# Gated linear attention ahead of two expert layers: gate sums on TensorE, whole query and score tiles, no products on GpSimd

## The chip, the cores and the metric

The kernel runs on one core of one Trainium2 chip. The metric is the time of one execution on the device in microseconds (us); the kernel before takes 743.27 us, the median of three runs between 742.84 and 743.48. In the profile the engines are called PE (TensorE, PEld its weight loads), DVE (VectorE), ACT (ScalarE), POOL (GpSimd) and SP (SyncE, which issues most DMAs).

## The reference

Three things are computed one after the other: a gated linear attention, and two top-1 expert layers on its rows. Only the first is touched.

```python
# q, k, v, f_logit: batch 4, heads 8, 768 tokens, 48 wide
f = 1.0 / (1.0 + np.exp(-f_logit))
for t in range(S):
    state = f[:, :, t, :, None] * state + einsum('bhd,bhe->bhde', k[:, :, t], v[:, :, t])
    y[:, :, t] = einsum('bhd,bhde->bhe', q[:, :, t], state)
x = y.transpose(0, 2, 1, 3).reshape(3072, 384)
x = moe(x, 8 experts, 384 -> 1024 -> 384, capacity)    # top-1, gated
x = moe2(x, 8 experts, 384 -> 1024 -> 384)             # top-1, gated
```

## The kernel before

The attention goes through 24 tiles of 128 tokens (six a batch), all eight heads of a tile at a time. A tile lies transposed: four head pairs beside each other, in each pair one head's 48 channels in partitions 0 to 47 and the other's in 64 to 111, the 128 tokens along the free axis. `X` holds gates, keys and queries of a tile in this form (3 x 4 x 128 float32 per partition); `Vn` and `R` hold the values in two natural layouts.

For a tile, with G the running sum of log(1 + exp(-f)) over its tokens, the chunked form is: `gates` (ScalarE) makes `L` = ln(1 + exp(-f)) in two activations; `decay` (VectorE) adds it up along the tokens with one scan (L372), held under a limit by the tile `caps` (L369); `expand` (ScalarE, L387 and L388) makes `eg` = exp(-G) and `ei` = exp(G). Queries times `eg` and keys times `ei` are the factors: the first head's query product (L389) and the key product `KD` (L390) on GpSimd, the second head's query product on VectorE in `keys` (L396). The first two tiles have L389 on VectorE, too. `T` is one tile of two planes, one for each head of a pair: the 64 partitions of the head hold its queries, the other 64 get its masked scores. `keys_t` transposes `KD` on TensorE and ScalarE copies it (`KT`); `scores` multiplies `KD` and `T` in quadrants of 64x64 (L416, L417), `masked` brings them through the causal mask into the other half of `T` in two instructions of 64x512 (L423); `updates` multiplies `KT` with `Vn` (`kv`), `states` (VectorE, L452 and L461) carries the state `S` on. `place` copies the states into `R` beside the values (ScalarE, L471 and L472), so that one product of 128 rows per head and chunk, 64x48 (L482), gives states and scores together in `y`. `rows`, `rows_t`, `rows_c` and `logits` copy the rows out, transpose them (`xp`, `xT`) and multiply by the gate weights (`rt`, L254).

The loop of 27 steps is software pipelined. The table `STAGES` gives the order in which a step issues its stages and how many tiles each lags behind; every engine runs its own instructions in that order. Per three tiles the routing adds some twenty tiny VectorE instructions (the one-hot choice `dla`, `oha`, the counts `cum`, the slots), which `step()` puts between the large ones. The weights of the first expert are split in two parts, `w0h` and `w0l`, on the way (`SPLITS`: behind which step, on which engine). SP issues all loads in order; X has four buffers, Vn three, R four.

After the loop a hand-written tail works off the last tiles and the first products of the first expert (`hpm`), and then both expert layers run as one sequence of groups, on TensorE mostly. If a chunk's decay leaves a safe range (`_guard`) a general path recomputes everything; it doesn't run here.

Of the kernel before, what the change touches and what calls it, by code (L numbers as in the profile page):

```python
# [22 lines left out]
DM = H * D  # L23
# [16 lines left out]
GMAX = 40.0  # L40
GCLAMP = 80.0
# [26 lines left out]
C_W = 360  # L68
# [125 lines left out]
def _route(*args, **kw):  # L194
# [9 lines left out]
# The engine of the weight splits behind a loop step of the attention: v(ector) or g(psimd).  # L204
SPLITS = {7: "v", 9: "g", 12: "g", 14: "g", 18: "g", 21: "g", 23: "g", 24: "v", 26: "gvvv"}
# Products by loop step that keep the tensor engine clocked up while the attention starts.
NWARM = (11, 1, 0, 0, 0, 11, 7, 3, 0, 0)

# What a loop step of the attention does, in each engine's order, and how many tiles behind.
STAGES = (  # L210
    ("place", 6),
    ("g_choose", 9),
    ("g_save", 13),
    ("decay", 3),
# [13 lines left out]
    ("keys", 3),  # L228
# [12 lines left out]
# in the first NFIRST steps with the next tile's gates behind the tile's own factors  # L241
# [4 lines left out]
# tiles with query factors from the vector engine, and tiles whose gates are loaded by themselves  # L246
NDVE = 2
NSPLIT = 2
# [16 lines left out]
def _scatter1(tc, key, dst, idx, src, bound):  # L265
    """Rows to places of their own: no two scatters of a key write the same row."""
    ins = tc.nc.gpsimd.indirect_dma_start(  # L267
        out=dst,
        out_offset=bass.IndirectOffsetOnAxis(ap=idx, axis=0),
        in_=src,  # L270
        in_offset=None,
        bounds_check=bound,
        oob_is_err=False,
    )
    ins = ins.ins
    tc.declare_no_dep(ins, group=key, reason="scatters to distinct rows")
    tc.add_to_no_dep_group(key, ins)
# [13 lines left out]
def _attention(tc, env, fkq, vn, vs, x1, tab1, early, masks, first, side, after, first_group):  # L291
    """Chunked attention, a tile of 128 tokens (two chunks) for all heads at a time, and the routing
    of its rows. Software pipelined: each loop step works on seven tiles, a stage apart."""
    nc = tc.nc
    with ExitStack() as ctx:
# [15 lines left out]
        caps = [e1.tile([P, NPAIR, P], F32, name=f"caps{i}") for i in range(2)]  # L311
        for c in caps:
            nc.vector.memset(c, GCLAMP)
        NVB = 3
        NXB = 4
        xbuf = [e1.tile([P, 3, NPAIR, P], F32, name=f"X{i}") for i in range(NXB)]
        tbuf = [b1.tile([P, 2, NPAIR, P], F32, name=f"T{i}") for i in range(4)]
        vbuf = [b1.tile([P, 2, DM], F32, name=f"Vn{i}") for i in range(NVB)]
        for vb in vbuf:
            nc.gpsimd.memset(vb[64:128, 0], 0.0)  # L320

        def load_x(i):
            t = tiles[i] = _Bag()
            t.X = xbuf[i % NXB]
            if i < NSPLIT:
                nc.sync.dma_start(out=t.X[:, 0], in_=fkq[i, :, 0])
                if i == 1:
                    masks()
                nc.sync.dma_start(out=t.X[:, 1:3], in_=fkq[i, :, 1:3])
            elif i < NXB:  # L330
                nc.sync.dma_start(out=t.X, in_=fkq[i])
# [11 lines left out]
        def load_vs(i):  # L343
            t = tiles[i]
            t.R = b4.tile([P, 2, 2, NPAIR * D], F32, name=f"R{i}", tag="R")
            nc.sync.dma_start(out=t.R[64:128, :, 0, :], in_=vs[i, 0])
            nc.sync.dma_start(out=t.R[0:64, :, 1, :], in_=vs[i, 1])

        # the first tile in halves, a step of each behind the other
        halves = lambda i: [slice(0, 2), slice(2, NPAIR)] if i == 0 else [slice(0, NPAIR)]  # L350

        def gates(i):
            t = tiles[i]
            t.L = e2.tile([P, NPAIR, P], F32, name=f"L{i}", tag="L")
            En = e2.tile([P, NPAIR, P], F32, name=f"En{i}", tag="En")
            for k, a in enumerate(halves(i)):
                col = NTILE if k else i
                nc.scalar.activation(
                    flat(En[:, a]), flat(t.X[:, 0, a]), AF.Exp, scale=-1.0, accum_out=env.esum[:, col : col + 1]
                )  # L360
                nc.scalar.activation(flat(t.L[:, a]), flat(En[:, a]), AF.Ln, bias=1.0)

        def decay(i):
            t = tiles[i]
            t.G = e2.tile([P, NPAIR, P], F32, name=f"G{i}", tag="G")
            # sums up to the limit; where a head pair starts, the limit is its own first term
            c = caps[i % 2]
            for a in halves(i):
                nc.vector.tensor_scalar(  # L369
                    out=c[:, a, 0:1], in0=t.L[:, a, 0:1], scalar1=GCLAMP, scalar2=None, op0=ALU.min  # L370
                )
                nc.vector.tensor_tensor_scan(  # L372
                    out=flat(t.G[:, a]), data0=flat(t.L[:, a]), data1=flat(c[:, a]), initial=0.0, op0=ALU.add, op1=ALU.min
                )
            step()
            step()

        def expand(i):
# [3 lines left out]
            t.T = tbuf[i % 4]  # L382
            t.KD = b2.tile([P, NPAIR, P], F32, name=f"KD{i}", tag="KD")
            # at first nothing else has work
            eng = nc.vector if i < NDVE else nc.gpsimd
            for a in halves(i):
                nc.scalar.activation(flat(t.eg[:, a]), flat(t.G[:, a]), AF.Exp, scale=-1.0)  # L387
                nc.scalar.activation(flat(t.ei[:, a]), flat(t.G[:, a]), AF.Exp)  # L388
                eng.tensor_tensor(out=t.T[0:64, 0, a], in0=t.X[0:64, 2, a], in1=t.eg[0:64, a], op=ALU.mult)  # L389
                nc.gpsimd.tensor_tensor(out=t.KD[:, a], in0=t.X[:, 1, a], in1=t.ei[:, a], op=ALU.mult)  # L390
            nc.gpsimd.tensor_copy(out=env.glast[:, i], in_=t.G[:, :, P - 1])

        def keys(i):
            t = tiles[i]
            for a in halves(i):
                nc.vector.tensor_tensor(  # L396
                    out=t.T[64:128, 1, a], in0=t.X[64:128, 2, a], in1=t.eg[64:128, a], op=ALU.mult
                )
# [1349 lines left out]
```

## Time and profile before

| what | us |
|---|---|
| time, median of three runs | 743.27 |
| span of the profiled execution | 737.6 |
| PE busy in the span | 664.8 |
| DVE busy | 467.8 |
| POOL busy | 393.2 |
| ACT busy | 327.9 |

The span goes from the first to the last instruction of the profiled execution; the time also takes in what lies around it. Busy times are of the whole span, in which the attention (to about 180 us) and the expert layers have different limits, so the rows below are taken by stretch. A busy TensorE is not one at its peak, and instructions that wait at a port count as busy.

### The profile page before, as it was taken

Reading aid. Unit: us, or ns where it says so; the run is one execution under the profiler, and the core shown is the slowest. Engines: PE = TensorE matmul, PEld = TensorE weight load, DVE = VectorE, ACT = ScalarE, POOL = GpSimd, SP = SyncE. Lnnn points to the kernel's source line nnn. Section 1 sums busy time; section 2 is a strip of 40 time slices with the busy share of each in tenths; the row PEclk is TensorE's granted clock in tenths of the full one; section 3 lists DMA queues with packets and bytes.
Section 4 is the critical chain, followed back from the end, with each engine's and each line's share of the span. In section 5 each row is a group of like instructions: output and inputs, shape, how many; then the busy total and the mean of one; then the engine's idle time right before and its main releaser. Section 6 shows DMA issues by size and latency. Waiting matters only on the chain.

```text
span 737.6 us, 15364 instructions
## 1 busy us (share of the span) xinstructions
PE 664.8 (90%) x5583; PEld 607.6 (82%) x5586; DVE 467.8 (63%) x1036; ACT 327.9 (44%) x702; POOL 393.2 (53%) x368
## 2 busy tenths in 40 slices
PE   7777686777889999999999899979999999999995
PEld 4556575666779899989999799869999899999995
DVE  8999999998558655574465755425545353555642
ACT  6566666665225443434434244115444343454431
POOL 4354757555446654645737454136765475756731
PEclk9899878789899999999999999999999999999998
DMA  9999999932348664655748161127544354544400
GB/s 265 247 213 212 180 188 199 168 101 80 93 115 221 183 160 98 152 87 169 147 144 171 48 204 40 31 74 252 152 136 127 105 159 121 164 141 134 130 23 20
DMA packets 61175, 104.27 MB, mean 141 GB/s; under 512 B 12444, under 2 KB 30462, under 8 KB 61091
## 3 DMA queue, kind: packets, MB, share of 16 engines
q1 hardware_dynamic: 53411, 87.63, 48.3%
q0 software_dynamic: 7680, 15.57, 7.7%
q8 instruction: 46, 0.75, 0.5%
q14 instruction: 38, 0.31, 0.2%
HBM read 88.21 MB, written 15.79 MB: 141 GB/s over the span
## 4 chain that ended last, share of the span: by engine, by line
PE 54%; DVE 19%; DMA 13%; issue 8%; POOL 2%; SPq 2%; ACT 1%; another core or an unknown queue 0%; DVEq 0%; POOLq 0%
PE hpm L1131 24%; PE ypm L1155 7%; PE ypm L1156 7%; PE ypm L1157 7%; DMA out_dram<-yr,tdm 5%; DVE T L396 4%; DVE T L423 3%; DMA X<-in_fkq_dram 3%; PE tpm L1108 2%; DVE dla L103 2%; DVE G L372 1%; DVE xT L511 1%; DMA raw<-in_w_dram 1%; DMA Vn<-in_vn_dram 1%; PE tym L896 1%
## 5 line engine op out<-in xcount | busy, mean ns | idle before, releaser
L1131 PE MATMUL hpm<-xhm,w0h 128*128 128x288 f32 (+11 forms) x456 | 155.6, 342 | 4.4 <-DVE hlm L1143 3.6
L1155 PE MATMUL ypm<-hhm,w1h 128*128 128x288 f32 (+11 forms) x456 | 155.0, 340 | 0.0
L1143 DVE SCALAR_TENSOR_TENSOR hlm<-hpm,hhm 128x288 fp32r<-128x288 f32 (+11 forms) x152 | 81.4, 536 | 115.7 <-ACT hhm L1142 89.3
L1156 PE MATMUL ypm<-hlm,w1h 128*128 128x288 f32 (+11 forms) x456 | 151.3, 332 | 0.0
L1157 PE MATMUL ypm<-hhm,w1l 128*128 128x288 f32 (+11 forms) x456 | 150.9, 331 | 0.0
L1142 ACT ACTIVATE hhm<-hpm 128x288 fp32r<-128x288 f32 (+11 forms) x152 | 72.5, 477 | 176.1 <-PE hpm L1131 160.9
L1131 PE MATMUL hpm<-xhm,w0l 128*128 128x288 f32 (+11 forms) x456 | 150.8, 331 | 0.0
L1131 PE MATMUL hpm<-xlm,w0h 128*128 128x288 f32 (+11 forms) x456 | 145.0, 332 | 0.0
L996 POOL TENSOR_TENSOR w0l<-raw,w0h 128x512 fp32r<-128x512 f32 x63 | 80.2, 1289 | 51.9 <-ACT w0h L995 51.4
L281 POOL DMA_INDIRECT xrm<-x,idcm x64 | 70.2, 1097 | 54.9 <-DVE valm L991 34.1
L996 POOL TENSOR_TENSOR w1l<-raw,w1h 128x512 fp32r<-128x512 f32 x60 | 77.0, 1298 | 34.6 <-ACT w1h L995 33.6
L1131 PEld LDWEIGHTS hpm<-xhm,w0h 128*128 128x128 f32 x456 | 86.8, 190 | 7.6 <-DVE hlm L1143 4.2
L1155 PEld LDWEIGHTS ypm<-hhm,w1h 128*128 128x128 f32 x456 | 86.9, 191 | 2.0
L1157 PEld LDWEIGHTS ypm<-hhm,w1l 128*128 128x128 f32 x456 | 86.7, 190 | 2.2
L1156 PEld LDWEIGHTS ypm<-hlm,w1h 128*128 128x128 f32 x456 | 86.9, 190 | 1.8
L1131 PEld LDWEIGHTS hpm<-xhm,w0l 128*128 128x128 f32 x456 | 86.7, 190 | 1.7
L1131 PEld LDWEIGHTS hpm<-xlm,w0h 128*128 128x128 f32 x456 | 85.6, 190 | 2.2
L267 POOL DMA_INDIRECT tab<-pos,sum x30 | 30.6, 1019 | 67.8 <-DVE sum L176 61.4
L389 POOL TENSOR_TENSOR T<-X,eg 64x512 f32<-64x512 f32 x22 | 28.2, 1283 | 63.7 <-ACT eg L387 55.1
L1116 ACT CAST xhm<-tpm 128x336 fp32r<-128x336 f32 (+8 forms) x64 | 25.2, 435 | 79.9 <-PE tpm L1108 76.8
L995 ACT CAST w0h<-raw 128x512 fp32r<-128x512 f32 x96 | 57.2, 616 | 2.5 <-DMA raw<-in_w_dram 2.3
L995 ACT CAST w1h<-raw 128x512 fp32r<-128x512 f32 x96 | 56.4, 621 | 0.0
(201 smaller groups left out, 1133.6 us busy)
## 6 DMA issues: line engine op xcount, KB each, us to landing
raw<-in_w_dram SPq DMA_DIRECT2D x192, 256.0 KB
X<-in_fkq_dram SPq DMA_DIRECT2D x40, 288.0 KB
x<-xr SPq DMA_DIRECT2D x8, 582.0 KB
Vn<-in_vn_dram SPq DMA_DIRECT2D x24, 192.0 KB
R<-in_vs_dram SPq DMA_DIRECT2D x48, 96.0 KB
Vn<-in_vn_dram SPq DMA_DIRECT2D x24, 96.0 KB
X<-in_fkq_dram SPq DMA_DIRECT2D x2, 768.0 KB
X<-in_fkq_dram SPq DMA_DIRECT2D x2, 512.0 KB
```

What stands on the lines that cost most here:

```text
L267: ins = tc.nc.gpsimd.indirect_dma_start(out=dst, out_offset=bass.IndirectOffsetOnAxis(ap=idx, axis=0), in_=src, in_offset=None, bounds_che ...
L281: nc.gpsimd.indirect_dma_start(out=dst, out_offset=None, in_=src, in_offset=bass.IndirectOffsetOnAxis(ap=idx, axis=0), bounds_check=bound, ...
L389: eng.tensor_tensor(out=t.T[0:64, 0, a], in0=t.X[0:64, 2, a], in1=t.eg[0:64, a], op=ALU.mult)
L396: nc.vector.tensor_tensor(out=t.T[64:128, 1, a], in0=t.X[64:128, 2, a], in1=t.eg[64:128, a], op=ALU.mult)
L995: nc.scalar.copy(out=hi, in_=raw)
L996: eng.tensor_tensor(out=lo, in0=raw, in1=hi.bitcast(F32), op=ALU.subtract)
L1131: nc.tensor.matmul(hp[:, :N], w[:, c, fs], x[:, c, :N], start=(k == 0), stop=(k == len(parts) - 1))
L1142: nc.scalar.activation(hh[:, :N], hp[:, :N], AF.Relu)
L1143: nc.vector.scalar_tensor_tensor(out=hl[:, :N], in0=hp[:, :N], scalar=0.0, in1=hh[:, :N].bitcast(F32), op0=ALU.max, op1=ALU.subtract)
L1155: nc.tensor.matmul(g.yp[d][:, :N], w2h[:, fc, ds_], hh[:, :N], start=(fc == 0), stop=False)
L1156: nc.tensor.matmul(g.yp[d][:, :N], w2h[:, fc, ds_], hl[:, :N], start=False, stop=False)
L1157: nc.tensor.matmul(g.yp[d][:, :N], w2l[:, fc, ds_], hh[:, :N], start=False, stop=(fc == NFC - 1))
```

## The change

- **Gate sums.** The gate inputs come untransposed, 128 tokens in the partitions (`F`, 192 KB a tile, a DMA of its own, three buffers). A new stage `bound` on VectorE holds them above -80. The two activations of `gates` run on 384 columns instead of 512. `sums` on TensorE replaces `decay`: four products per tile with a triangular matrix of ones (`C_INC` in the constants) leave G transposed in PSUM, in the same two buffers (tag `tr`) that the transposes `kp` and `xp` use. The scan and `caps` go.
- **Factors.** `factors` on VectorE makes the whole query tile `QT` (128x512) and the whole key tile `KD` (128x512, with ei held under a limit in the same instruction). `expand` keeps its two activations, now from PSUM; GpSimd's products and the stage `keys` go. GpSimd keeps the small copy `glast`.
- **Scores and outputs.** The scores of both heads stay in their own quadrants, and `masked` is one instruction of 128x512 into a tile `SC`. The output has, per pair and chunk, one product of `QT` with block-diagonal states `RS` and one of `SC` with block-diagonal values `RV`, 64x96 each, added up in PSUM: sixteen products of 96 columns in place of sixteen of 48. The zero blocks are set once by GpSimd memsets at the start; `RS` has two buffers, `RV` three.
- **Splits.** All twelve weight splits of the attention are on GpSimd, one behind each of the steps 7, 9, ... 23, 24, 25, 26; four were on VectorE, three of these behind step 26.
- **Small things.** No halves for the first tile; the constants `cs` grow from 360 to 488 columns and are loaded behind the first gates; the guard compares exp(-G).

The core of the diff (removed comments and unchanged stages left out):

```diff
-SPLITS = {7: "v", 9: "g", 12: "g", 14: "g", 18: "g", 21: "g", 23: "g", 24: "v", 26: "gvvv"}
+SPLITS = {7: "g", 9: "g", 11: "g", 13: "g", 15: "g", 17: "g", 19: "g", 21: "g", 23: "g", 24: "g", 25: "g", 26: "g"}
 STAGES = (
     ("place", 6),
+    ("bound", 2),
...
-    ("decay", 3),
+    ("sums", 3),
...
-    ("keys", 3),
+    ("factors", 3),
...
+        fbuf = [e1.tile([P, DM], F32, name=f"F{i}") for i in range(3)]
+        xbuf = [e1.tile([P, 2, NPAIR, P], F32, name=f"X{i}") for i in range(NXB)]
+        sbuf = [b1.tile([P, 2, 2, NPAIR * D], F32, name=f"RS{i}") for i in range(2)]
+        rbuf = [b1.tile([P, 2, 2, NPAIR * D], F32, name=f"RV{i}") for i in range(NRB)]
...
+            nc.sync.dma_start(out=t.F, in_=fn[i])
...
                 for u in (0, 64):
-                    nc.sync.dma_start(out=t.X[u : u + D], in_=fkq[i, u : u + D])
+                    nc.sync.dma_start(out=t.X[u : u + D], in_=kq[i, u : u + D])
...
+        def bound(i):
+            t = tiles[i]
+            nc.vector.tensor_scalar(out=t.F, in0=t.F, scalar1=FMIN, scalar2=None, op0=ALU.max)
...
-                nc.vector.tensor_tensor_scan(
-                    out=flat(t.G[:, a]), data0=flat(t.L[:, a]), data1=flat(c[:, a]), initial=0.0, op0=ALU.add, op1=ALU.min
-                )
+            t.G = p_2.tile([P, NPAIR, P], F32, name=f"G{i}", tag="tr")
+            for a in range(NPAIR):
+                nc.tensor.matmul(
+                    t.G[:, a],
+                    t.L[:, 2 * a : 2 * a + 2].rearrange("p h d -> p (h d)"),
+                    env.cs[:, C_INC : C_INC + P],
+                    start=True,
+                    stop=True,
                 )
...
-                eng.tensor_tensor(out=t.T[0:64, 0, a], in0=t.X[0:64, 2, a], in1=t.eg[0:64, a], op=ALU.mult)
-                nc.gpsimd.tensor_tensor(out=t.KD[:, a], in0=t.X[:, 1, a], in1=t.ei[:, a], op=ALU.mult)
+        def factors(i):
+            t = tiles[i]
+            t.QT = b4.tile([P, NPAIR, P], F32, name=f"QT{i}", tag="QT")
+            t.KD = e2.tile([P, NPAIR, P], F32, name=f"KD{i}", tag="KD")
+            nc.vector.tensor_tensor(out=t.QT, in0=t.X[:, 1], in1=t.eg, op=ALU.mult)
             step()
+            nc.vector.scalar_tensor_tensor(
+                out=t.KD, in0=t.ei, scalar=EIMAX, in1=t.X[:, 0], op0=ALU.min, op1=ALU.mult
+            )
             step()
...
+                    for q in (slice(0, 64), slice(64, 128)):
+                        nc.tensor.matmul(sc[q, a, h], t.KD[q, a, u], t.QT[q, a, u], start=True, stop=True)
...
-                            t.y[u, hh * D : (hh + 1) * D],
-                            t.T[:, par, a, u],
-                            t.R[:, h, par, a * D : (a + 1) * D],
-                            start=True,
-                            stop=True,
+                            t.y[u, 2 * a * D : (2 * a + 2) * D].rearrange("p (h e) -> p h e", h=2),
+                            t.SC[:, a, h] if k else t.QT[:, a, u],
+                            (t.RV if k else t.RS)[:, h, :, e],
+                            start=k == 0,
+                            stop=k == 1,
                         )
```

How a step's instructions stand on the engines, in the middle of the loop. First VectorE, one whole step of the kernel before; `t4a`, `sea` belong to the routing, and L372 is the scan.

```order
L369 TENSOR_SCALAR caps_184<-L_1593 128x4
L372 SCALAR_TENSOR_TENSOR G_1651<-L_1593,caps_184 128x512
L423 TENSOR_TENSOR T_193<-sc_1659,cs 64x512 x2
L396 TENSOR_TENSOR T_194<-X_190,eg_1678 64x512
L156 TENSOR_TENSOR t4a_1709<-rt_1210,lim 128x24
L511 COPY xT_1711<-xp_1704 128x384
L141 TENSOR_REDUCE sea_1713<-exa_1608 128x3
L452 TENSOR_TENSOR S_1643<-kv_1686,S_1643 128x384
L160 SCALAR_TENSOR_TENSOR t4a_1709<-t4a_1709,rt_1210 128x24
L461 TENSOR_TENSOR S_1744<-S_1643,eg_1464 128x192
```

The same step of VectorE in the changed kernel:

```order
L360 TENSOR_SCALAR F_184<-F_184 128x384
L423 TENSOR_TENSOR SC_1721<-sc_1704,cs 128x512
L396 TENSOR_TENSOR QT_1753<-X_189,eg_1727 128x512
L160 TENSOR_TENSOR t4a_1756<-rt_1239,lim 128x24
L398 SCALAR_TENSOR_TENSOR KD_1754<-ei_1728,X_189 128x512
L145 TENSOR_REDUCE sea_1759<-exa_1725 128x3
L512 COPY xT_1761<-xp_1749 128x384
L164 SCALAR_TENSOR_TENSOR t4a_1756<-t4a_1756,rt_1239 128x24
L452 TENSOR_TENSOR S_1678<-kv_1732,S_1678 128x384
```

The scan, its clamp and one mask product have gone from the step, `bound` and `KD` have come in, and `QT` is twice as many partitions as the product that it replaces.

On GpSimd a step of the kernel before (two products, the copy, a weight split, and the memset of a row's spare columns):

```order
L389 TENSOR_TENSOR T_194<-X_190,eg_1678 64x512
L390 TENSOR_TENSOR KD_1680<-X_190,ei_1679 128x512
L391 COPY glast<-G_1651 128x4
L996 TENSOR_TENSOR w0l_604<-raw_391,w0h_603 128x512
L495 MEMSET xr_1762 128x3x4
```

And two steps of the changed kernel there (`tab` is the list of the experts' tokens, `sua` the slots):

```order
L390 COPY glast<-eg_1502 128x4
L269 DMA tab_62<-tokid,sua_1534 30720x1 x2
L390 COPY glast<-eg_1611 128x4
L269 DMA tab_62<-tokid,sua_1534 30720x1
L997 TENSOR_TENSOR w0l_621<-raw_406,w0h_620 128x512
```

Both products have moved to VectorE; the copies, the scatters of the routing and the splits are left.

TensorE, one step of the changed kernel (the outputs `y` are eight rows like the last but one):

```order
L376 MATMUL G_1920<-cs,L_191 128x128 x4
L418 MATMUL sc_1931<-QT_1858,KD_1859 64x64 x16
L440 MATMUL kv_1957<-Vn_192,KT_1874 64x96 x8
L504 MATMUL xp_1969<-cs,xr_1807 128x128 x3
L407 MATMUL kp_1985<-cs,KD_1859 128x128 x4
L483 MATMUL y_1992<-RS_195,QT_1632 64x96 x2
L256 MATMUL rt_1909<-xT_1981,wg1s 32x128 x3
```

and the end of a step of the kernel before (`kv` of a batch's last tile, which has half the columns; `lts` is the routing's copy of the logits):

```order
L440 MATMUL kv_1472<-Vn_197,KT_1397 64x48 x8
L503 MATMUL xp_1487<-cs,xr_1435 128x128 x3
L405 MATMUL kp_1497<-cs,KD_1357 128x128 x4
L482 MATMUL y_1504<-R_1312,T_193 64x48 x16
L260 MATMUL rt_1210<-cs,lts_1481 128x96 x3
L254 MATMUL rt_1535<-xT_1494,wg1s 32x128 x3
```

The sums stand at the head of the step, right behind the logits of the step before, and the outputs stream 96 columns instead of 48; the rest keeps its place.

## Rows read from the trace of the kernel before

**Rows 1.** The page: span, and busy us, share and instructions by engine.

```profile
span 737.6 us, 15364 instructions
PE 664.8 (90%) x5583; PEld 607.6 (82%) x5586; DVE 467.8 (63%) x1036; ACT 327.9 (44%) x702; POOL 393.2 (53%) x368
```

**Rows 2.** Stretches: length; busy us of PE, PEld, DVE, ACT, POOL; clock, DMA share, GB/s.

```profile
0.00:30.60 30.60, 24.32 (x271) 15.79 (x276) 26.43 (x50) 17.86 (x39) 12.62 (x25) 0.89 0.98 268
30.60:164.00 133.40, 96.59 (x1709) 80.82 (x1705) 126.95 (x236) 86.46 (x183) 75.06 (x79) 0.85 0.92 182
237.00:737.00 500.00, 482.64 (x2944) 456.28 (x2942) 263.02 (x600) 193.44 (x412) 267.72 (x230) 0.99 0.46 124
```

**Rows 3.** Timeline of ScalarE, start and duration: gates of tiles 5 and 23.

```profile
30.62 0.61 ACT L358 ACTIVATE En<-X 128x512 f32<-128x512 f32 x1
163.97 0.63 ACT L358 ACTIVATE En<-X 128x512 f32<-128x512 f32 x1
```

**Rows 4.** Waits from 30.6 to 164 us: total, times, longest.

```profile
ACT R L471 <- DVE S L452: 33.1, 18, 2.4
PE rt L254 <- DVE xT L511: 32.6, 16, 3.2
```

**Rows 5.** VectorE's groups, 30.6 to 164 us: count | busy us, mean ns | idle before.

```profile
L396 DVE TENSOR_TENSOR T<-X,eg 64x512 f32<-64x512 f32 x18 | 27.6, 1533 | 0.6
L423 DVE TENSOR_TENSOR T<-sc,cs 64x512 f32<-64x512 f32 x37 | 25.5, 689 | 2.1 <-PE sc L417 1.2
L372 DVE TENSOR_TENSOR_SCAN G<-L,caps 128x512 f32<-128x512 f32 x18 | 22.0, 1225 | 1.8
L103 DVE TENSOR_TENSOR dla<-lsa,mxa 128x24 f32<-128x24 f32 x5 | 10.6, 2125 | 0.2
L511 DVE COPY xT<-xp 128x384 f32<-128x384 f32 x18 | 9.9, 551 | 0.1
...
L150 DVE TENSOR_TENSOR cum<-cum,oha 128x8 bf16<-128x8 bf16 x12 | 7.5, 621 | 0.0
...
L369 DVE TENSOR_SCALAR caps<-L 128x4 f32<-128x4 f32 x18 | 3.0, 164 | 0.0
...
L996 DVE TENSOR_TENSOR w0l<-raw,w0h 128x512 fp32r<-128x512 f32 x1 | 0.7, 684 | 0.0
```

**Rows 6.** Timelines of VectorE and GpSimd: one product alone, one beside GpSimd's, `dla` alone.

```profile
127.43 0.69 DVE L396 TENSOR_TENSOR T<-X,eg 64x512 f32<-64x512 f32 x1
156.45 2.37 DVE L396 TENSOR_TENSOR T<-X,eg 64x512 f32<-64x512 f32 x1
155.74 1.29 POOL L389 TENSOR_TENSOR T<-X,eg 64x512 f32<-64x512 f32 x1 [3.39 <-ACT eg L387]
157.00 1.27 POOL L390 TENSOR_TENSOR KD<-X,ei 128x512 f32<-128x512 f32 x1
184.68 0.18 DVE L103 TENSOR_TENSOR dla<-lsa,mxa 128x24 f32<-128x24 f32 x1
```

**Rows 7.** Timeline of TensorE in one step at the upper clock.

```profile
113.83 0.42 PE L254 MATMUL rt<-xT,wg1s 128*32 128x128 f32 x6 [1.19 <-DVE xT L511]
115.25 0.88 PE L440 MATMUL kv<-Vn,KT 128*64 128x96 f32 x16
116.98 1.14 PE L482 MATMUL y<-R,T 128*64 128x48 f32 x32
```

**Rows 8.** The same at the lower clock, in other steps.

```profile
122.78 1.55 PE L440 MATMUL kv<-Vn,KT 128*64 128x96 f32 x16
128.85 0.65 PE L254 MATMUL rt<-xT,wg1s 128*32 128x128 f32 x6 [2.09 <-DVE xT L511]
```

**Rows 9.** DMA share, 30.6 to 164 us in 40 slices; X's issues, first and last start.

```profile
DMA  9999999999999699999979999989999998700870
...
L335 SPq DMA_DIRECT2D X<-in_fkq_dram x40: 315/326/1368, 11.5 to 142.2; - x40
```

**Rows 10.** Timeline of VectorE at the loop's end: three weight splits.

```profile
176.48 1.89 DVE L996 TENSOR_TENSOR w1l<-raw,w1h 128x512 fp32r<-128x512 f32 x3
```

More of the change, by code (lines that the diff above doesn't have):

```diff
@@ L39 @@
 FILL = 1 << 20
-GMAX = 40.0
-GCLAMP = 80.0
+EGMIN = float(np.exp(-40.0))
+FMIN = -80.0
+EIMAX = float(np.exp(80.0))
 EMAX = 1e15
@@ L67 @@
 C_B1, C_B2, C_SEL = 336, 344, 352
-C_W = 360
+C_INC = 360
+C_W = 488
 RAWC = 512
@@ L288, in _gather1, with _attention @@
     )
-def _attention(tc, env, fkq, vn, vs, x1, tab1, early, masks, first, side, after, first_group):
+def _attention(tc, env, fn, kq, vn, vs, x1, tab1, early, masks, first, side, after, first_group):
     nc = tc.nc
@@ L344, in load_vs @@
             t = tiles[i]
[L345 to L350, printed above, removed]
+            t.RV = rbuf[i % NRB]
+            nc.sync.dma_start(out=t.RV[0:64, :, 0, :], in_=vs[i, 0])
+            nc.sync.dma_start(out=t.RV[64:128, :, 1, :], in_=vs[i, 1])
@@ L363, in decay @@
[L363 to L370, printed above, removed]
-                )
-                nc.vector.tensor_tensor_scan(
-                    out=flat(t.G[:, a]), data0=flat(t.L[:, a]), data1=flat(c[:, a]), initial=0.0, op0=ALU.add, op1=ALU.min
-                )
-            step()
-            step()
+            En = e2.tile([P, DM], F32, name=f"En{i}", tag="En")
@@ L381, in expand @@
             t.ei = e2.tile([P, NPAIR, P], F32, name=f"ei{i}", tag="ei")
[L382 to L388, printed above, removed]
-                eng.tensor_tensor(out=t.T[0:64, 0, a], in0=t.X[0:64, 2, a], in1=t.eg[0:64, a], op=ALU.mult)
-                nc.gpsimd.tensor_tensor(out=t.KD[:, a], in0=t.X[:, 1, a], in1=t.ei[:, a], op=ALU.mult)
-            nc.gpsimd.tensor_copy(out=env.glast[:, i], in_=t.G[:, :, P - 1])
-        def keys(i):
-            t = tiles[i]
[L395 to L398, printed above, removed]
+            nc.scalar.activation(flat(t.eg), flat(t.G), AF.Exp, scale=-1.0)
+            nc.scalar.activation(flat(t.ei), flat(t.G), AF.Exp)
+            nc.gpsimd.tensor_copy(out=env.glast[:, i], in_=t.eg[:, :, P - 1])
+        def factors(i):
+            t = tiles[i]
+            t.QT = b4.tile([P, NPAIR, P], F32, name=f"QT{i}", tag="QT")
+            t.KD = e2.tile([P, NPAIR, P], F32, name=f"KD{i}", tag="KD")
+            nc.vector.tensor_tensor(out=t.QT, in0=t.X[:, 1], in1=t.eg, op=ALU.mult)
+            step()
+            nc.vector.scalar_tensor_tensor(
+                out=t.KD, in0=t.ei, scalar=EIMAX, in1=t.X[:, 0], op0=ALU.min, op1=ALU.mult
+            )
             step()
@@ L415, in scores @@
                     u = slice(h * 64, h * 64 + 64)
-                    nc.tensor.matmul(sc[64:128, a, h], KD[0:64, a, u], T[0:64, 0, a, u], start=True, stop=True)
-                    nc.tensor.matmul(sc[0:64, a, h], KD[64:128, a, u], T[64:128, 1, a, u], start=True, stop=True)
+                    for q in (slice(0, 64), slice(64, 128)):
+                        nc.tensor.matmul(sc[q, a, h], t.KD[q, a, u], t.QT[q, a, u], start=True, stop=True)
         def masked(i):
             t = tiles[i]
-            for lo, pl in ((64, 0), (0, 1)):
-                q = slice(lo, lo + 64)
-                nc.vector.tensor_tensor(
-                    out=t.T[q, pl].rearrange("p a (h t) -> p (a h) t", h=2),
-                    in0=t.sc[q].rearrange("p a h t -> p (a h) t"),
-                    in1=mask[q],
-                    op=ALU.mult,
-                )
-                step()
+            t.SC = b3.tile([P, NPAIR, 2, 64], F32, name=f"SC{i}", tag="SC")
+            nc.vector.tensor_tensor(
+                out=t.SC.rearrange("p a h t -> p (a h) t"),
+                in0=t.sc.rearrange("p a h t -> p (a h) t"),
+                in1=mask,
+                op=ALU.mult,
+            )
+            step()
         def updates(i):
@@ L470, in place @@
             t = tiles[i]
-            nc.scalar.copy(out=t.R[0:64, :, 0, :], in_=t.S[0:64, 0:2])
-            nc.scalar.copy(out=t.R[64:128, :, 1, :], in_=t.S[64:128, 0:2])
+            t.RS = sbuf[i % 2]
+            nc.scalar.copy(out=t.RS[0:64, :, 0, :], in_=t.S[0:64, 0:2])
+            nc.scalar.copy(out=t.RS[64:128, :, 1, :], in_=t.S[64:128, 0:2])
         def output(i, pool=p_1, tag="y"):
@@ L477, in output @@
             for a in range(NPAIR):
-                for par in range(2):
-                    hh = 2 * a + par
+                e = slice(a * D, (a + 1) * D)
+                for k in range(2):
                     for h in range(2):
@@ L605, in _attention @@
             f.__name__: f
-            for f in (load_x, load_v, load_vs, gates, decay, expand, keys, keys_t, scores, masked, updates, states, place,
+            for f in (load_x, load_v, load_vs, bound, gates, sums, expand, factors, keys_t, scores, masked, updates, states, place,
                       output, rows, rows_t, rows_c, logits, g_copy, g_turn, g_choose, g_rank, g_store, g_save, g_list, warm, lead)
@@ L1594, in first_group @@
             return begin, lambda j: M.turn(g0, j, "sc"), lambda j: M.divide(g0, j), product, parts
-        _attention(tc, env, fkq, vn, vs, x1, tab1, early, load_masks, first, side, after, first_group)
+        _attention(tc, env, fn, kq, vn, vs, x1, tab1, early, load_masks, first, side, after, first_group)
         env.t_h = "h"
@@ L1688, in _layout, with transposed @@
 def _layout(x):
-    def transposed(a, pad):
+    def transposed(a):
         a = a.reshape(B, NPAIR, 2, TPB, P, D).transpose(0, 3, 2, 5, 1, 4)
-        z = np.full((B, TPB, 2, 64, NPAIR, P), pad, np.float32)
+        z = np.zeros((B, TPB, 2, 64, NPAIR, P), np.float32)
         z[:, :, :, :D] = a
```

51 lines of the change are left out of this document (24 added, 27 removed).

## The prediction

> **What bounds the kernel now.** I read the page first [rows 1], then cut the span into stretches [rows 2]. From 237 us on TensorE is busy 482.6 of 500 us: that is the expert layers, which the change doesn't touch. Between 30.6 and 164 us, the steady part of the attention loop, TensorE is busy 96.6 of 133.4 us, ScalarE 86.5 and GpSimd 75.1, but VectorE 126.95: 95%. The two ends of this stretch are the gates of tile 5 and of tile 23 [rows 3], 18 loop steps apart, so a step takes 133.35 / 18 = 7.41 us. The waits agree: TensorE waits 32.6 us for the tile `xT`, ScalarE 33.1 us for the state `S`, both from VectorE [rows 4]. The time is VectorE's queue, step by step, and 7.05 us of each 7.41 are its instructions.
>
> What fills it stands in [rows 5]. The product `T<-X,eg` takes 1533 ns in the mean, although one takes 0.69 us when it is alone and 2.37 us when GpSimd's products run beside it [rows 6]: in that row the two GpSimd products (1.29 and 1.27 us from 155.74 on) fill the very time that VectorE's product needs to finish. The same shows on tiny instructions: `dla` 2125 ns in the mean against 0.18 us alone [rows 5, 6], `cum` 621 ns against the 0.17 us or so of its neighbours. So part of VectorE's load is waiting behind GpSimd, counted as busy.
>
> **The change, part by part** (sums over the 18 steps).
>
> VectorE loses the scan (22.0 us), the clamp `caps` (3.0), `T<-X,eg` (27.6) and, as the mask becomes one instruction over 128 partitions, 18 of 37 mask products of 689 ns (12.4) [rows 5]. With no products on GpSimd the excess on `dla` (10.6 - 5 x 0.18 = 9.7) and `cum` (7.5 - 12 x 0.17 = 5.5) goes too. That is 80.2 us. It gains two products of 128x512 per tile, `QT` and `KD`; the split `w0l`, a product of just this shape with both inputs in SBUF, takes 684 ns [rows 5], as the one of 64x512 does, so I price both at 0.69 us: 24.8 us. It gains the clamp `bound` on 128x384: between a tiny instruction (164 ns, `caps`) and a copy of 128x384 out of PSUM (551 ns, `xT`) [rows 5]; I take 0.35 us, 6.3 in sum. Of the weight splits that stay on GpSimd nine fall into these steps; each could hold one VectorE product by up to 2.37 - 0.69 = 1.68 us, 0 to 15 in sum, and I take half, 7.6. New load: 127.0 - 80.2 + 38.7 = 85.5 us, 4.75 us a step. VectorE is then no longer what a step waits for, so the rest of its saving is worth nothing and the next limit decides.
>
> TensorE is the next one. A step at the full clock runs from 113.83 us (`rt`) to the end of `y` at 118.12 [rows 7]: 4.3 us with hardly a gap. The triangular product adds eight matmul records of 128x128 with float32 operands; six such records take 0.42 us (`rt`), so 0.56. The outputs keep their 32 records, but each streams 96 columns in place of 48: sixteen records of that width take 0.88 us (`kv`), 32 of them 1.76 less the tail that is paid once, some 1.5 against 1.14 now: +0.4. With the routing's small products in some steps (about 0.3) a step needs 5.6 us at 2.4 GHz. At 1.2 GHz the same rows read 0.65 and 1.55 [rows 8], a factor of 1.55 to 1.76; 5.6 becomes about 9.5. The granted clock of the stretch is 0.85 [rows 2], 30% of the time at the lower level: steps per us 0.7 / 5.6 + 0.3 / 9.5 = 0.157, or 6.4 us a step. But the lower level is granted today after TensorE has idled behind `xT` [rows 4], and that idle time shrinks; where it hardly idles the clock is 0.99 [rows 2]. So 5.6 to 6.4; I take 6.2, nearer the upper end, because the engines now hand work to each other within a step with little slack: sums on TensorE, two exponentials on ScalarE, two products and the copy `xT` on VectorE, then the logits that stand ahead of the next sums in TensorE's queue. Added from rows that is 0.56 + 2 x 0.63 + 2 x 0.69 + 0.55 + 0.42 = 4.2 us, and ScalarE's three copies and VectorE's routing steps stand in the same queues. ScalarE itself stays at about 86.5 / 18 = 4.8 us, and the `tr` buffers in PSUM, now used three times a step, make the transposes `kp` wait for the second exponential, which lies ahead of them anyway.
>
> DMA carries the same bytes per tile (the gates leave the 576 KB of X as 192 KB of their own). Its share is 0.92 of the stretch [rows 2], so 6.8 us of a step, yet the gates don't wait for it: the last X is issued at 142.2 us and its gates run at 163.97 [rows 3, 9]. These 22 us of lead can be used up once; at 6.2 us a step the lead shrinks by 22 us x (1 - 6.2 / 7.41) plus what the transfers lag, and something is left. I cost it at nothing here; it is a rival below.
>
> What else moves: the two steps left of the loop after tile 23's gates gain as the others do, 2 x 1.2 = 2.4 us. The three VectorE splits of 1.89 us at the loop's end [rows 10] are spread over earlier steps on GpSimd: -1.0, since part of that time lay beside TensorE. Three outputs in the tail cost 0.4 more each: +1.1. The start is held by the first loads, nearly the same bytes: 0. GpSimd's ten extra memsets at the start lie beside those loads and cost nothing.
>
> Sum: 18 x (7.41 - 6.2) = 21.8, + 2.4 + 1.0 - 1.1 = 24.1 us off. The profiled execution's span is 737.6 us, 5.7 below the median of 743.27; I take those 5.7 us as unchanged: a span of about 713.5 and a time of **719 us**.
>
> **The rivals.**
>
> (a) *The clock comes up.* With the idle behind `xT` gone TensorE keeps the upper level, a step takes 5.6 to 5.8 us: 18 x 1.7 = 30.6, + 3 = 34 off, 709 us. For: 0.99 in the stretch in which TensorE is busy 97% [rows 2]. Against: a stage of 85 to 90% is not that. The Trainium skill, page TensorE: Matmul & The Clock Gate, section What's actually happening, says that the throttled state is the default and activity releases it; by that rule (a) would be the forecast.
>
> (b) *DMA takes over.* If the lead can't be used up, because a load may start only when its buffer comes free, a step takes what the queues need: 6.8 us less what the gates gain by landing in all 128 partitions. The first stretch, where loads into 128 partitions dominate, moved 268 GB/s at a share of 0.98, the steady one 182 at 0.92 [rows 2]: 273 against 198 at full share, 0.27 us less for 197 KB. So 6.5 to 6.8: 18 x 0.61 to 0.91 = 11 to 16 off and 2 more: 725 to 730 us. For: the slices show hardly a free one [rows 9]. The Trainium skill, page SBUF — State Buffer, section Door 1: The DMA port swizzle, gives 196 GB/s into 64 partitions of one half and 328 into all 128 for 1 MiB; by these the gates gain 0.4 us, an estimate from that page, and the step is 6.4.
>
> (c) *TensorE becomes the bound at the lower clock*, and the kernel slower: at 9.5 us a step 18 x 2.1 = 38 us are lost, 781 us. It decides from the point where the lower level fills f of the time with (1 - f) / 5.6 + f / 9.5 = 1 / 7.41, f = 0.59, a mean granted clock of 0.70. The stretch shows 0.85. Milder mixtures land just above 743.
>
> (d) *It doesn't relieve VectorE*: the two products of 128x512 cost more than 0.69 us or collide with every split, and the chain within the step adds up: a step of 7.2 to 7.5 us, 739 to 745 us.
>
> **How the numbers follow.** The forecast (steps of 6.0 to 6.4 us, 714 to 724 us) 0.47; (a) 0.18; (b) 0.20; (d) 0.09, of it 0.03 within 0.2% and 0.02 above; (c) 0.06. 0.2% is 1.5 us, about what a measurement of this kernel can tell from no change. Faster: 0.47 + 0.18 + 0.20 + 0.04 = 0.89; same 0.03; slower 0.08. The range takes all of the forecast, most of (a) and all of (b) with a margin: 708 to 734 us.
>
> **What would show it.** In the changed kernel's profile the gates of tiles 5 and 23 should lie about 112 us apart, VectorE be busy some 75 to 80% between them, `QT` and `KD` near 0.7 us each, `bound` under 0.55, `y` near 1.5 us for its 32 records and the sums 0.55 at the upper clock. TensorE's idle time before `rt` should be mostly gone. If (b) holds, the exponential of the gates or `bound` waits for `F`, or the products for X; if (a), the granted clock reads above 0.95; if (c), under 0.7. From the loop's end on, everything should be the same, only earlier. Wrong would be a loop that still takes 7 us a step while no engine is busy over 85%: then I have misjudged the chain between the queues.

## The result and the profile after

The changed kernel takes **721.25 us** (median of four executions, 719.9 to 722.44), against 743.06 us for the kernel before on the same chip, some 21.8 us less; the ratio was estimated at 0.9715, 95% interval 0.969 to 0.974. The profiled execution took 722.44 us, the longest of the four. Its span is 720.6 us, so 1.84 us lie around it. The other kernels of the study show the same 1.8 us, and executions of the kernel before too (a span of 739.0 us in a time of 740.88).

The page of the kernel after, to be held against [rows 1]: span, and busy us, share and instructions by engine; then the granted clock by slice, where 9 is 90% or more.

```profile
span 720.6 us, 15672 instructions
PE 681.4 (95%) x5778; PEld 623.1 (86%) x5778; DVE 395.7 (55%) x999; ACT 322.7 (45%) x697; POOL 342.9 (48%) x338
...
PEclk9999999989999999999999999999999999999997
```

VectorE lost 72 us, GpSimd 50; TensorE gained 17, and its mean granted clock rose from 0.95 to 0.98. What bounds the attention now is seen between the gates of tiles 5 and 23, the stretch of [rows 3]. The timeline of ScalarE has the two gates:

```profile
28.88 0.52 ACT L366 ACTIVATE En<-F 128x384 f32<-128x384 f32 x1
...
147.69 0.52 ACT L366 ACTIVATE En<-F 128x384 f32<-128x384 f32 x1
```

They are 118.81 us apart, 6.60 us a step; before it was 133.35 and 7.41. The same stretch by engines (columns as in [rows 2]: length; busy us of PE, PEld, DVE, ACT, POOL; granted clock, DMA share, GB/s):

```profile
28.88:147.69 118.81, 110.92 (x1899) 94.31 (x1895) 78.22 (x218) 83.80 (x183) 32.77 (x46) 0.98 0.95 203
```

VectorE fell from 95% to 78.22 / 118.81 = 66%. TensorE stands at 93%, the transfers at a share of 0.95. Of the waits of [rows 4], TensorE's for `xT` is gone and ScalarE's for `S` is down from 33.1 to 5.4 us. The longest waits now are these (total, times, longest); in the first two VectorE and GpSimd stand idle until there is work for them:

```profile
DVE SC L423 <- PE sc L418: 31.3, 19, 3.9
POOL glast L390 <- ACT eg L388: 29.7, 15, 5.7
POOL xr L496 <- DMA x<-xr: 14.9, 3, 8.4
POOL w0l L997 <- ACT w0h L996: 14.2, 5, 3.7
ACT xr L498 <- DMA x<-xr: 11.8, 3, 5.0
DVE QT L396 <- ACT eg L388: 7.8, 4, 3.3
...
PE xp L504 <- ACT xr L498: 6.3, 4, 2.9
...
ACT RS L472 <- DVE S L452: 5.4, 9, 0.8
```

In fourteen of the eighteen steps hardly anything holds TensorE up. Every third one from tile 13 on is long (8.27, 10.07, 8.41, 10.53 us): a group of three tiles begins there, GpSimd clears and ScalarE fills its row buffer `xr` (L496, L498), and of these there are three, so the save of the rows of three groups ago must have landed. The chain of waits through one such step (start, us, what) shows whole transfers and then the copy:

```profile
68.06 6.37 DMA raw<-in_w_dram
74.44 8.15 DMA x<-xr
82.67 0.48 ACT xr L498
83.15 0.50 ACT eg L388
83.65 0.50 ACT ei L389
84.19 0.66 PE kp L407 x4
84.84 1.47 PE y L483 x32
```

Of the span's 17.0 us (737.6 to 720.6), 1.74 are the start (the gates of tile 5 at 28.88 and not 30.62), 14.54 the stretch, 0.7 all that follows. Both spans are of single executions, that of before 3.8 us under its median and that of after 1.2 above; the medians differ by 21.8.

### The profile page after: what moved, and what is told of

Its sections match the earlier page's. It is cut to its first block, busy times and chain, and to the rows that moved or that the text cites. A ratio compares the mean times of both kernels' runs of the same rounds, so it can differ in the third digit from the quotient of the medians.

```text
span 720.6 us, 15672 instructions
## 1 busy us (share of the span) xinstructions
PE 681.4 (95%) x5778; PEld 623.1 (86%) x5778; DVE 395.7 (55%) x999; ACT 322.7 (45%) x697; POOL 342.9 (48%) x338
## 4 chain that ended last, share of the span: by engine, by line
PE 51%; issue 17%; DMA 13%; POOL 10%; DVE 4%; ACT 2%; SPq 1%; POOLq 0%; DVEq 0%; ACTq 0%
PE hpm L1132 19%; PE ypm L1156 6%; PE ypm L1157 6%; PE ypm L1158 6%; DMA X<-in_kq_dram 4%; DMA x<-xr 3%; POOL w0l L997 3%; POOL w1l L997 3%; PE y L483 3%; POOL tab L269 2%; PE G L376 2%; POOL xrm L283 2%; DMA tab<-pos,sum 2%; PE tpm L1109 2%; PE tym L972 2%
## 5 line engine op out<-in xcount | busy, mean ns | idle before, releaser
L997 POOL TENSOR_TENSOR w0l<-raw,w0h 128x512 fp32r<-128x512 f32 x64 | 82.1, 1299 | 66.3 <-ACT w0h L996 65.7
L997 POOL TENSOR_TENSOR w1l<-raw,w1h 128x512 fp32r<-128x512 f32 x64 | 82.4, 1302 | 42.5 <-ACT w1h L996 41.7
L997 DVE TENSOR_TENSOR w0l<-raw,w0h 128x512 fp32r<-128x512 f32 x32 | 44.0, 1377 | 13.8 <-ACT w0h L996 11.9
```

The source lines that it names most:

```text
L997: eng.tensor_tensor(out=lo, in0=raw, in1=hi.bitcast(F32), op=ALU.subtract)
```

## Experiments: the transfers

**Theory A**: the row buffers cost the long steps; more of them, or an earlier save, would give that time back. **Theory B**: the transfers as a whole have no time left, and the row buffers are only where that shows.

**Two more row buffers.**

```diff
+xe = [e1.tile([P, RG, W], F32, name=f"xe{i}") for i in range(2)]
...
-grp["xr"] = b3.tile([P, RG, W], F32, name=f"xr{i}", tag="xr")
+early_xr = 3 <= i // RG < 5
+grp["xr"] = xe[i // RG - 3] if early_xr else b3.tile([P, RG, W], F32, name=f"xr{i}", tag="xr")
```

> The changed kernel with two more row buffers `xr` (groups 3 and 4 of tiles get one of their own each, so that a buffer comes back after five groups and not three). Theory A (the row buffers: copying rows of a group waits until the save of three groups ago has landed): the long steps, which stand at every third tile from tile 13 on and cost 14.0 us above the 5.82 us of the other fourteen, go; gates of tile 5 to tile 23 in 105 to 110 us in place of 118.8, time 707 to 713 us. Rival B (the DMA queues have no time left, share 0.96; the row buffers are only where it shows): the wait moves to X, F or the values, 114 us or more between the two gates, 716 to 721 us.

Measured: 716.39 us (714.03 to 721.03), some 5 us off; in the profiled execution, the longest of its five, tiles 5 and 23 are 111.53 us apart, and no wait for a save is left. What follows tile 23's gates took 579.5 us in this execution, 6.6 more than in the kernel after, so here the stretch says more than the time. VectorE's `bound` now waits for `F` instead:

```profile
28.19:139.72 111.53, 109.25 (x1889) 93.53 (x1887) 76.22 (x214) 84.85 (x183) 30.23 (x46) 0.98 0.96 212
...
DVE F L361 <- DMA F<-in_fn_dram: 7.8, 6, 2.3
```

The time lies at the lower edge of B's forecast, the stretch between the two. With the same bytes a step is 6.20 us. The stretch of the kernel after lies 10.8 us above what TensorE needs (108.02 us, shown below), and 7.3 of these are gone here: most of the wait was the buffers' own in these two executions, and the rest moved to the next transfer, as B has it. One long step is left (9.36 us, at tile 19), and the transfers' share is 0.96 against 0.95.

**The save a step earlier.**

```diff
-    ("g_save", 13),
+    ("g_save", 12),
```

> The changed kernel with the save of a group's rows issued one loop step earlier (12 steps behind in place of 13), buffers as they are. Theory A (row buffers): a step of 5.8 us more between issue and reuse takes that much from each of the four waits of 2.5 to 4.7 us: 708 to 714 us, nearly what two more buffers give. Rival B (DMA has no time left): the same transfers in nearly the same order, 717 to 721 us.

Measured: 718.69 us (713.11 to 721.24). That decides nothing by itself: the median is B's, the shortest execution A's. In the profiled one, the longest of the four, the stretch is 117.97 us, and `bound` waits 20.9 us for `F` from 30 to 140 us, where the kernel after has 1.2 (30.6 to 147.7 us):

```profile
DVE F L360 <- DMA F<-in_fn_dram: 20.9, 11, 3.9
...
POOL xr L496 <- DMA x<-xr: 7.2, 3, 5.0
```

The wait for the save is half of what it was, the rest of it moved, and the stretch is hardly shorter.

**Fewer bytes, buffers as they were.**

```diff
-            nc.gpsimd.memset(vb[64:128, 0], 0.0)
+            nc.gpsimd.memset(vb[:, 0], 0.0)
...
-            nc.sync.dma_start(out=t.Vn[0:64, 0], in_=vn[i, 0:64])
```

> The changed kernel without the second load of the values' first 64 rows (98 KB of some 1245 KB that a loop step moves; that part of the operand is set to zero once, so the state in the middle of a tile is left out). Row buffers and the save's place as they are. Theory A (row buffers): the save waits behind a little less, the four long steps stay, each shorter by about 0.5 us: 716 to 720 us. Rival B (DMA has no time left): 8% of the 107 us that the queues were busy between tiles 5 and 23, 8.5 us off: 711 to 714 us.

Measured: 713.74 us (709.94 to 716.43), B's forecast. With three row buffers still, all four long steps are gone, and of the waits for a save one of 2.7 us is left:

```profile
27.19:135.13 107.94, 107.19 (x1890) 92.19 (x1887) 76.60 (x214) 84.64 (x183) 30.76 (x46) 1.00 0.91 206
...
POOL xr L495 <- DMA x<-xr: 2.7, 1, 2.7
```

So fewer bytes are enough by themselves: with 8% fewer the save lands in time, and three buffers do. As more buffers took back most of the time too, the long steps come from both together, transfers this dense and a save that has only three buffers to land in. The row also gives the floor below them: TensorE busy 107.19 of 107.94 us at a clock of 1.00, **6.0 us a step**. One thing isn't separated: the load left out is also one of the seven that SP issues per tile. On SP's timeline the issues fill some 82 of the 118.81 us in the kernel after and 68 of 107.94 here, so SP isn't busy throughout; a part of it in the waits is not excluded.

**The same load replaced by a copy.** The values are in the same partitions already, in the other half of the buffer `Vn`, so GpSimd can copy them. This kernel leaves out the last tile's copy, so that its state in the middle is built from an older tile's values; the next has it.

```diff
+    ("copy_v", 4),
...
-            nc.sync.dma_start(out=t.Vn[0:64, 0], in_=vn[i, 0:64])
+        def copy_v(i):
+            t = tiles[i]
+            nc.gpsimd.tensor_copy(out=t.Vn[0:64, 0], in_=t.Vn[0:64, 1])
```

> The changed kernel without the second load of the values' first 64 rows; GpSimd copies them in place of it (64x384, in its idle time). If the bytes of that load are what counted, it gives what leaving the load out gave: 711 to 716 us. If the copy on GpSimd collides with VectorE's products or stands in the way of the weight splits: 717 us or more.

Measured: 712.56 us (711.85 to 713.49), the forecast for bytes; in its trace one long step is left (8.50 us, at tile 15). Beside it on the same chip the changed kernel as it is:

> The changed kernel as it is, beside the next ones: 719 to 723 us, with its long steps at every third tile again.

Measured: 722.34 us (719.0 to 724.27), its long steps again at every third tile from tile 13 (7.80, 9.24, 8.63, 9.99). So the copy gives 9.8 us.

**Copy and buffers together.**

> The changed kernel with both: GpSimd copies the values' first 64 rows (for the last tile too), and two more row buffers. Theory B (bytes): with the load gone hardly a wait is left that the buffers could shorten (stretch from 110.0 to 108 us, TensorE's 6.0 us a step): 709 to 713 us. Theory A (the buffers are a cost of their own): the 5 us that they gave alone come on top, 706 to 708 us.

Measured: **709.40 us** (708.54 to 712.09), 0.9558 of the kernel before (0.9504 to 0.9611), and faster than both kernels of this case. That is at the lower end of B's forecast; the buffers add about 3 us to the copy (709.40 against 712.56, measured in different sets of runs). The stretch is TensorE's alone:

```profile
27.42:135.44 108.02, 107.30 (x1891) 92.31 (x1888) 78.39 (x214) 84.70 (x184) 39.67 (x64) 1.00 0.90 208
```

**Half of the second value set copied too.**

```diff
-            nc.sync.dma_start(out=t.RV[0:64, :, 0, :], in_=vs[i, 0])
...
+            nc.sync.dma_start(out=t.RV[0:64, 1, 0, :], in_=vs[i, 0, :, 1])
...
+            nc.gpsimd.tensor_copy(out=pair(t.RV[0:64, 0, 0, :]), in_=v[0:64, 0])
+            nc.gpsimd.tensor_copy(out=pair(t.RV[64:128, 1, 1, :]), in_=v[64:128, 1])
```

> As the kernel before it, and half of each tile's second set of values is copied on GpSimd instead of loaded (98 KB fewer per tile again, in two copies of 64x192). Theory B with TensorE as the floor: the stretch can't go below 18 x 6.0 = 108 us, only the start, where the loads are dense, may gain 1 or 2 us: 708 to 712 us. Rival G (GpSimd, which does its work in order, now waits for the values' load and holds up what follows): 714 us or more.

Measured: 734.26 us, widely scattered (723.89, 732.76, 735.76, 762.13), but the shortest of them is still 14 us above the kernel before it. In size that is rival G; the wait is another one than it named. The transfers' share falls to 0.61 in the profiled execution (735.76 us), and nothing comes of it: the second copy of a step stands 24.8 us in all until a scatter issued ahead of it has landed, by what the profile infers, and as GpSimd works in order, TensorE's `kv` waits for the copy `Vn` behind it. Why this copy waits for the scatter, when two others right behind the scatter don't, the traces do not show.

```profile
29.85:153.21 123.36, 114.23 (x1891) 98.17 (x1888) 77.66 (x214) 84.51 (x183) 52.27 (x100) 0.93 0.61 160
...
POOL RV L364 <- DMA tab<-tokid,sua: 24.8, 7, 6.1
...
PE kv L448 <- POOL Vn L355: 8.7, 3, 3.3
```

## Experiments: the engines

**Sums twice.**

```diff
-            for a in range(NPAIR):
+            for a in [*range(NPAIR), *range(NPAIR)]:
```

> The changed kernel with each tile's triangular sums computed twice: one more group of eight 128x128 records, 1.09 us of TensorE per step at the upper clock. Theory B (between tiles 5 and 23 the transfers set the pace at some 6.6 us a step, TensorE alone would need 6.0): the step becomes TensorE's 7.1 us and the long steps vanish under it, 18 x (7.1 - 6.6) = 9 us and 1 to 3 for the steps outside: 730 to 734 us. Rival E (the waits of the long steps add to TensorE's time, whatever it is): 24 x 1.09 = 26 us, 743 to 748 us.

Measured: 732.18 us (729.89 to 734.67), B's forecast; 9.8 us more than the kernel after in the same set. The long steps are gone: a step is 123.28 / 18 = 6.85 us, and TensorE is busy throughout. The second sums cost it (122.91 - 107.30) / 18 = 0.87 us a step and not the 1.09 put in: sixteen records take 1.98 us from the start of `G` to that of `sc`, where eight take 1.09 (shown further below).

```profile
49.44 2.05 PE L376 MATMUL G<-cs,L 128*128 128x128 f32 x16
51.42 1.15 PE L418 MATMUL sc<-QT,KD 64*64 64x64 f32 x32
...
32.22:155.50 123.28, 122.91 (x2035) 108.06 (x2032) 76.64 (x214) 85.48 (x183) 29.70 (x46) 1.00 0.83 193
```

The step is thus the longer of TensorE's need and the transfers'; their waits do not add up. That excludes rival E, which at 0.87 us would still be 24 x 0.87 = 21 us.

**Sums in one record each** (operands in float32r, on top of the kernel with the copies of half of the second set):

```diff
-        lbuf = [e1.tile([P, H, 64], F32, name=f"L{i}") for i in range(2)]
...
+        linc = b1.tile([P, P], F32R, name="linc")
+        lbuf = [e1.tile([P, H, 64], F32R, name=f"L{i}") for i in range(2)]
...
-                    env.cs[:, C_INC : C_INC + P],
+                    linc,
```

> As the kernel before it, with the sums' operands held as float32r, so that a triangular product is one record in place of two (the sums are rounded more coarsely by that). Theory H (TensorE is the floor once the transfers have time): four records of 0.14 us in place of eight, 0.55 us less a step: 18 x 0.55 and 2 to 3 outside, 12 us less, 697 to 701 us. Rival I (the hand-over between the engines within a step, VectorE's `xT` first, is next at once): 3 us less or nothing, 706 to 711 us.

Measured: 722.07 us (717.85 to 725.02). Neither forecast: its base is held up by GpSimd's copies (the same wait, 20.4 us here). What it does show is the price: the sums are four records and take 0.59 us from their start to that of `sc`, and the seven steps from tile 5 to tile 12, which the copies don't yet delay, take 38.84 us against 42.31 in the kernel after: 0.50 us less each. What it would give on the kernel with the first copy alone was not tried. TensorE's timeline there:

```profile
49.03 0.66 PE L387 MATMUL G<-linc,L 128*128 128x128 f32 x4
49.62 0.39 PE L429 MATMUL sc<-QT,KD 64*64 64x64 f32 x6
```

**More work on VectorE.**

```diff
+        junk = e1.tile([P, NPAIR, P], F32, name="junk")
...
+            for _ in range(2):
+                nc.vector.tensor_tensor(out=junk, in0=t.X[:, 1], in1=t.eg, op=ALU.mult)
```

> The changed kernel with two more products of 128x512 on VectorE behind `KD` in each step, 2 x 0.68 = 1.37 us of work that nobody reads (about what the scan, 1.22 us a step, was). Theory C (VectorE at 68% has room): VectorE goes to 85% of the stretch, the time moves by 0 to 4 us, 720 to 725 us. Rival F (what follows in VectorE's queue, `xT` and the state, is on the path of each step): up to 24 x 1.37 = 33 us, 738 to 754 us.

Measured: 734.00 us (731.49 to 736.9), 11.7 us more than the kernel after. Theory C as I put it falls: VectorE is busy 96.29 of 129.28 us, 74%, and yet a step is 0.66 us longer than in the kernel after on the same chip (117.42 us).

```profile
28.50:157.78 129.28, 111.48 (x1860) 93.96 (x1859) 96.29 (x252) 83.21 (x184) 31.17 (x46) 0.97 0.86 191
...
ACT RS L475 <- DVE S L455: 34.5, 18, 3.6
...
PE rt L256 <- DVE xT L515: 14.9, 17, 2.6
```

These are the two waits of [rows 4] come back. VectorE has idle time, but ahead of the masks (in the kernel after it waits 31.3 us there for the scores `sc`); between `KD` and `xT` it has little, and what is put there is half paid by the step. It is not the full price of rival F either.

**The key product on GpSimd again.**

```diff
-            nc.vector.scalar_tensor_tensor(
-                out=t.KD, in0=t.ei, scalar=EIMAX, in1=t.X[:, 0], op0=ALU.min, op1=ALU.mult
-            )
+            nc.gpsimd.tensor_tensor(out=t.KD, in0=t.X[:, 0], in1=t.ei, op=ALU.mult)
```

> The changed kernel with the key product `KD` on GpSimd again (as a plain product: the clamp of `ei` is left out), `QT` on VectorE. Theory C (TensorE and the transfers set the step now; VectorE, 68% busy, has room): `QT` beside it rises from 0.68 to 2.0 to 2.4 us, VectorE stays below 85%, and the step grows only by what `KD` lands later, 0 to 0.4 us: 721 to 729 us. Rival D (the shared port was what the step of before was made of): the step goes back by 0.8 to 1.2 us as `KD`, the scores and all small operations wait behind GpSimd: 735 to 743 us.

Measured: 721.62 us (718.25 to 725.13), theory C's forecast: no difference that can be seen in the time. In the profiled execution (719.67 us) the stretch is 121.37 us, 2.6 to 4 more than in the two profiled executions of the kernel after, with the long steps still in it; so a few us are not excluded. As the transfers could have hidden it, the same edit was put on the best kernel:

> The first kernel of this set with the key product `KD` on GpSimd (a plain product, the clamp of `ei` left out), to see what the product there costs when the transfers no longer hide it. Theory C (GpSimd's products cost nothing while VectorE has room): 709 to 715 us. Rival D (it was hidden behind the transfers): `QT` at 1.1 us in place of 0.7 and `KD` at 1.4, 0.4 us or more later each step, 18 x 0.4 = 7: 717 us or more.

Measured: 711.57 us (710.29 to 712.91), theory C's forecast again, 2.2 us more than without it, ranges overlapping. `QT` beside the product on GpSimd takes 1328 ns in the mean from 30 to 140 us (683 in the kernel after), and the stretch grows by 1 us to 109.00:

```profile
L401 DVE TENSOR_TENSOR QT<-X,eg 128x512 f32<-128x512 f32 x18 | 23.9, 1328 | 0.0
```

So VectorE does slow down beside GpSimd, as in [rows 6], but at most a few us hang on it here. The difference to the run with more work on VectorE is the sum: `QT` gets 0.65 us longer, and `KD` with its 0.68 leaves VectorE's queue ahead of `xT`. VectorE is busy 77.64 us of the stretch, against 78.39 without the product on GpSimd, so this run doesn't try a fuller queue.

## Why the prediction held, step by step

The time, 719 against 721.25, the direction and the range are right; several terms are not, and some cancel. That the time comes within 2.3 us is in part luck: between the two profiled executions the stretch gave 14.5 us where 21.8 were forecast, and the medians lie 4.8 us further apart than these two executions do.

**VectorE's load.** Right in kind: forecast 85.5 us for 18 steps, measured 78.22. `QT` and `KD` take what was read from [rows 5], 683 and 682 ns against 0.69. `bound` takes 0.354 in the median against 0.35, 0.469 in the mean, for some wait behind GpSimd. The waits behind the splits, put at 7.6 us, came to about 5: some 2 on `bound`, some 3 on the tiny `t6a`.

```profile
L396 DVE TENSOR_TENSOR QT<-X,eg 128x512 f32<-128x512 f32 x18 | 12.3, 683 | 4.5 <-ACT eg L388 4.5
L398 DVE SCALAR_TENSOR_TENSOR KD<-ei,X 128x512 f32<-128x512 f32 x18 | 12.3, 682 | 0.0
...
L360 DVE TENSOR_SCALAR F<-F 128x384 f32<-128x384 f32 x18 | 8.4, 469 | 1.3 <-DMA F<-in_fn_dram 1.2
...
L169 DVE TENSOR_TENSOR t6a<-t4a,oha 128x24 f32<-128x24 f32 x5 | 4.1, 822 | 0.0
```

(VectorE's groups from 30.6 to 142 us.)

**TensorE's need.** The step at the upper clock was forecast at 5.6 us and is 6.0. The term that was mis-sized is the sums, 0.56 us. The timeline of TensorE in an undisturbed step:

```profile
47.46 0.60 PE L407 MATMUL kp<-cs,KD 128*128 128x128 f32 x4
...
49.86 0.42 PE L256 MATMUL rt<-xT,wg1s 128*32 128x128 f32 x6
50.21 1.16 PE L376 MATMUL G<-cs,L 128*128 128x128 f32 x8
51.30 1.09 PE L418 MATMUL sc<-QT,KD 64*64 64x64 f32 x30
```

From the start of `G` to that of `sc` it is 1.09 us for eight records. I had taken the price of `rt`, whose stationary operand is 128x32; the sums' is 128x128, as that of the transposes `kp`, whose four records take 0.60. 5.6 + 0.53 is 6.1. The outputs were right: `y` takes 1.47 us in the chain, forecast 1.5.

**The clock.** Rival (a) had this part: where nothing holds TensorE up, the granted clock is 1.00 (the best kernel's stretch), with 0.98 in the kernel after, against 0.85 in [rows 2]. The forecast mixed in 30% at 1.2 GHz for 6.4 us and took 6.2. So 6.2 was nearly TensorE's 6.0 for a wrong reason: too cheap a sum, too low a clock. The Trainium skill (TensorE: Matmul & The Clock Gate, What's actually happening) says that activity releases the throttled state; the traces agree, and the forecast should have followed them, since the row with 0.99 was before me.

**The transfers.** They were costed at nothing; this is the step of the argument that failed. Its reason was the 22 us of lead that the loads had, and most of that lead held: the last `F` is issued at 131.6 us, 16 us ahead of tile 23's gates, and `bound` waits 1.2 us in all for `F`. What had no such lead is the save of the rows. From tile 13 on engines wait for it, and the stretch is 118.81 us where TensorE needs 108.02 (the best kernel), so 10.8 us. Of these 7.2 are idle time of TensorE (7.89 us against 0.72), and 3.6 more busy time (110.92 against 107.30), at least in part at the lower clock that it is granted after such a wait: 1.00 from 100 to 104 us, 0.64 from 104 to 108. One sees it at the end of the long step at tile 16: TensorE has idled 2.36 us for `xr`, and `kp` takes 1.11 us then, against the 0.60 above.

```profile
L336 SPq DMA_DIRECT2D F<-in_fn_dram x24: 328/529/1857, 0.7 to 131.6; - x24
...
104.25 0.55 PE L504 MATMUL xp<-cs,xr 128*128 128x128 f32 x3 [2.36 <-ACT xr L498]
105.24 1.11 PE L407 MATMUL kp<-cs,KD 128*128 128x128 f32 x4 [0.44 <-ACT ei L389]
```

Rival (b) named the transfers, with a step of 6.5 to 6.8 us, and the step of 6.60 is its; the total is between its 725 to 730 and the forecast. But 6.5 to 6.8 is not what the queues need: with two more row buffers the same bytes took 6.20 us a step. It looked for the wait at `F` or X. That it would come at the save of the rows, which holds the row buffers, was nowhere in the text; [rows 9] show only loads. The Trainium skill (SBUF — State Buffer, Door 1: The DMA port swizzle) has a transfer into all 128 partitions faster than one into 64 of a half; by that the gates' new layout should help. The steady rate did rise, from 182 to 203 GB/s at shares of 0.92 and 0.95, about 8% at equal share; how much of that the layout gave was not measured.

**What lies around.** The two last loop steps, the splits and the tail were to give 2.3 us, and after the gates of tile 23 the kernel is 0.7 us shorter; the start gave 1.74 where none was counted. And the 5.7 us around the span were misread: 1.84 lie around it, and the profiled execution of before was 3.8 us faster than the median shown. As only the saving was used, and taken from the median in effect, this did no harm: 24.1 us forecast, 21.8 measured.

**The other rivals.** (c) didn't come, the clock rose; (d) neither, but the run with more work on VectorE shows how near it is: 1.37 us more in the wrong place bring [rows 4] back. That taking the products off GpSimd mattered by itself isn't borne out: with one of the two back, and VectorE's load the same, the time hardly changes; both were not tried. As far as the runs show, the gain came from VectorE's whole load going below TensorE's; which of scan, clamp, products and merged masks was decisive in before was not tested.

## What to carry to other kernels

When one engine's queue bounds a loop, price the next two limits below it and take the longest: here TensorE at 6.0 us and the transfers at 6.2 to 6.6, by the buffers that they had, stood under VectorE's 7.4, and the change was worth the distance to the nearer one. A DMA share of 0.9 with nobody waiting doesn't say that the transfers keep up once the loop gets faster: cost them at their own pace, and look at stores that hold buffers as well as at loads, since each has a lead of its own. Bytes that are on the chip already are cheapest to drop, as long as the engine that copies them doesn't stand behind a slow instruction of its own queue.

## What the runs showed of the hardware

- A float32 product of 128x128 with a 128x128 stationary operand is two records. Eight records take 1.09 us to the start of the next group and sixteen 1.98, so 0.11 us a record and some 0.2 us once. With a stationary operand of 128x32 a record takes some 0.06 us (0.35 us from `rt` to `G` for six). In float32r a product is one record, 0.59 us for four.
- A single product on GpSimd makes VectorE's product beside it 1.33 us long in the mean, 0.68 alone; before, two of them one behind the other made it 2.37 [rows 6].
- The save of 582 KB took 8.2 and 10.3 us in the kernel after, from its issue to the wait that it ended, while the loads ran beside it; that is longer than a whole step.
